# A backward pass with a state-space convolution and a feed-forward: the feed-forward spread more thinly over the table chain, one fold earlier, and two groups of loads further ahead

## The chip, the cores and the metric

The kernel runs on one core of one Trainium2 chip. The metric is the device time of one execution in microseconds (us), smaller is better. The engines are called PE (TensorE), DVE (VectorE), ACT (ScalarE), POOL (GpSimd) and SP (SyncE, here only an issuer of transfers); PEld is PE's loading of weights. To evacuate a result is to copy it out of the buffer in which PE left it. The granted clock is the share of its full speed that PE was given, and the DMA share is the mean busy share of the core's 16 DMA engines. L422 is line 422 of that kernel's source; the change adds lines.

## The reference, cut to what matters

The forward function is `x + s * silu(ffn(xn))`, where `xn` is the layer norm of `x`, `s` is a long convolution of `xn` with taps made from a diagonal state-space model, and `ffn` has two matrix products around a silu. The kernel returns the output and the gradients for the eleven differentiated inputs.

```python
def _A_ref(u, A_re, A_im, B_re, B_im, C_re, C_im, log_dt, Dskip):   # u: 1 x 2048 x 512, 128 states
    logdA = dt * (A_re + 1j * A_im)
    P = jnp.exp(logdA[:, :, None] * l[None, None, :])
    K = jnp.einsum("dn,dnl,dn->dl", Cc, P, dB).real                 # the taps
    ...                                                             # y = irfft(rfft(u) * rfft(K)) + u * Dskip
def _B_ref(x, w1, w2):                                              # 512 -> 1792 -> 512
    h = _silu(jnp.einsum("bsd,df->bsf", x, w1))
    return jnp.einsum("bsf,fd->bsd", h, w2)
xn = _layernorm(x)
out = x + _A_ref(xn, ...) * _silu(_B_ref(xn, B_w1, B_w2))
_out, _vjp = jax.vjp(_f, A_u, ..., B_x)                             # and all gradients for grad_out
```

## The kernel before

The 512 channels are worked on in four blocks `b`. For each block, `gen_tables` makes sines (ACT `sn`), multiplies them (DVE `E`), contracts them on PE (`ps_k`, then `ps_e`) and stores the taps `Kd`. `gen_conv_x` and `gen_conv_fwd` then do the convolution as a two-stage Fourier transform on PE: a first stage from `TF` (L286), a transposition by DMA from `dA` to `dB`, a second stage from `F` (L297, L298), a product of the spectra on DVE (`cm`, `sp_in`), and an inverse of two stages (L310, L319), from which DVE makes `S_b`. All these are Python generators. The order in which their steps are drawn is the order in which instructions enter each engine's queue.

```python
LAG = 3
def dft_fwd(k, w8, U, ev):
    ...                                                     # first stage into ps_s1, ev() to A
        nc.sync.dma_start_transpose(B[:, c], A[:, c]...)    # dB <- dA
    for _ in range(LAG):
        yield                                               # steps of others come in between
    ...                                                     # second stage, matmuls on B
```

`paced` draws one step of the chain and `rate` steps of another generator. The feed-forward has 72 steps: 8 chunks, each with seven steps of the first layer (`ps_h`, 8 matmuls) and two of the second (`ps_o`, 14 matmuls).

```python
def chain():
    yield from woven([gen_tables(k, 0), gen_conv_x(k, 0)], [2, 1])
    for b in range(1, 4):
        yield from woven([gen_tables(k, b), gen_conv_x(k, b), gen_conv_fwd(k, b - 1)], [3, 1, 1])
ffn = gen_ffn_fwd(k)
paced(chain(), ffn, 0.62)
...
gates = gen_gate_rows(k, ...)                                # ds = grad * silu(ffn), and the gate's gradient
interleave([gen_conv_fwd(k, 3), ffn, gates], [1, 3, 1])      # the last convolution: "the hole"
...
paced(bwd, woven([ffb, out], [2, 1]), BR)                    # backward convolution
...
ssm = gen_ssm_bwd(k, sb)                                     # state-space backward
paced(ffb, ssm, SR)
run(out)
...
interleave([ssm, chained([gen_dw2(k, fw), gen_dw1(k, fw)]), after(8, gen_ln_bwd(k, fw))], [2, 1, 2])
```

The state-space backward begins with loads of six parameters by transposing DMA, then a fold of block 0 (`GE` loaded, 23 matmuls, `Gf`), then the transposed table `YT`; the first product `ps_v` needs `Gf` (through `Gb`) and `YT`.

```python
par = load_params(k, sb, 0, k.D)
...
gf[0] = ssm_fold(k, 0, sb)
yt[0] = ssm_turned(k, *groups[0], sb)
```

`gen_out` writes the output rows. Its buffer for `x` is single, and the load stands in the step that uses it. `gen_ln_bwd` loads one step ahead.

```python
x = pool.tile([P, 2, k.D], BF16, name="go_x", tag="go_x", bufs=1)
nc.sync.dma_start(x[:], k.x_v[:, 2 * c:2 * c + 2, :])
...
q, pend = [load(0)], None                                    # gen_ln_bwd
for c in range(n + 1):
    if c + 1 < n:
        q.append(load(c + 1))
```

## Time and profile before

The median was 732.17 us over four runs (731.42 to 733.55). The profiled execution spans 732.4 us with a granted PE clock of 0.931. These moments, read from the lists of the instructions that touch one tile, carry the argument:

| moment (start of the instruction) | us |
|---|---|
| last matmuls of the last table (`ps_e`) | 254.6 |
| load of the last taps (`Kb`) issued | 263.7 |
| last `S_b` (last convolution done) | 313.9 |
| first `ps_da` (feed-forward backward) | 320.4 |
| last `du_b` (backward convolution done) | 468.0 |
| first `ps_v` (state-space products) | 490.7 |
| last `ps_da` | 536.0 |
| last state-space sum (`psS` copied) | 669.9 |
| end | 732.4 |

The view of waits gives, for an engine and line, what it waited for, then total us, number of times, longest. In the chain (40 to 262 us) two of its lines for the kernel before are:

```profile
DVE E L422 <- ACT sn L419: 18.2, 8, 5.3
...
ACT Xr L44 <- PE ps_k L447: 10.1, 8, 4.1
```

A time line has start, duration, engine, source line, operation, result and operand, shapes, count, and in brackets the idle time just before and what ended it.

### The profile page before, as it was taken

The numbers are of one execution on the slowest core, as the hardware profiler recorded it, in microseconds if no ns is written. First come the engines' busy times: TensorE is split into PE (matmuls) and PEld (weight loads), VectorE is DVE, ScalarE is ACT, GpSimd is POOL, SyncE is SP. The second block draws the span as 40 slices with busy tenths as digits, with TensorE's granted clock in tenths as the row PEclk, the third lists the DMA queues.
The fourth block names the chain that finished last, engine by engine and source line by source line (L and its number), as shares of the span: only waits on it lengthen the run. The fifth ranks groups of instructions, "written<-read, shape, count | busy, mean of one in ns | idle before, by whom it ended". The sixth has DMA issues, their size and how long they took to land.

```text
span 732.4 us, 13901 instructions
## 1 busy us (share of the span) xinstructions
PE 598.3 (82%) x5459; PEld 430.0 (59%) x5500; DVE 551.6 (75%) x1070; ACT 495.8 (68%) x671; POOL 107.7 (15%) x180
## 2 busy tenths in 40 slices
PE   0768968869999965569798799978797978899895
PEld 0535646555675643456576576647576646566784
DVE  6969996959988859877895989756897897784100
ACT  6768858769889866949679596646746767561211
POOL 2172200000010025600000000000002103102210
PEclk9877989989999995869999999999999999999998
DMA  9877847769669976579987875589959999930782
GB/s 291 304 172 195 264 170 211 273 171 280 277 183 281 338 266 162 183 162 261 322 203 233 242 224 180 160 197 210 249 156 295 253 286 280 217 120 28 155 179 66
DMA packets 207042, 159.26 MB, mean 217 GB/s; under 512 B 129024, under 2 KB 185344, under 8 KB 203392
## 3 DMA queue, kind: packets, MB, share of 16 engines
q1 hardware_dynamic: 193856, 135.29, 69.4%
q0 software_dynamic: 6224, 18.10, 6.9%
q10 hardware_dynamic: 6896, 4.98, 2.2%
q8 instruction: 43, 0.70, 0.4%
q14 instruction: 23, 0.19, 0.1%
HBM read 65.14 MB, written 62.26 MB: 174 GB/s over the span
## 4 chain that ended last, share of the span: by engine, by line
issue 52%; DVE 5%; POOL 5%; DMA 3%; PE 0%; ACT 0%; POOLq 0%; ACTq 0%; SPq 0%; DVEq 0%
POOL out_dram L939 1%; DMA out_dram<-gout 1%; DMA out_dram<-o 1%; DVE YD L599 1%; POOL out_dram L816 1%; DMA Kd<-KE 1%; DMA Gr<-in_grad_out_dram 1%; DVE ds L595 1%; DVE sp_in L332 1%; POOL out_dram L631 1%; POOL out_dram L958 1%; POOL out_dram L996 1%; POOL g L598 0%; DVE YD L603 0%; DVE YD L601 0%
## 5 line engine op out<-in xcount | busy, mean ns | idle before, releaser
L44 ACT CAST dA<-ps_s 128x1024 bf16<-128x1024 f32 x96 | 94.4, 1038 | 22.5 <-PE ps_s L286 13.2
L893 PE MATMUL ps_da<-doT,W 128*128 128x256 bf16 x448 | 62.7, 286 | 5.1 <-ACT doT L44 2.9
L541 PE MATMUL ps_h<-XT,W 128*128 128x256 bf16 x448 | 63.5, 293 | 1.5 <-ACT hT L44 0.8
L310 PE MATMUL ps_i<-I,sp_in 128*128 128x256 bf16 x384 | 53.4, 284 | 13.4 <-ACT dK L44 7.2
L558 PE MATMUL ps_o<-W,aT 128*128 128x512 bf16 x209 | 54.7, 394 | 4.1 <-ACT aT L549 2.9
L44 ACT CAST o<-ps_w 128x256 bf16<-128x256 f32 (+1 forms) x42 | 18.5, 441 | 57.2 <-PE ps_w L954 41.7
L44 ACT CAST dB<-ps_i 128x1024 bf16<-128x1024 f32 x48 | 47.2, 1025 | 12.0 <-PE ps_i L310 9.7
L746 DVE TENSOR_TENSOR Tp<-Vb,Eb 128x1344 bf16<-128x1344 bf16 x64 | 52.3, 852 | 3.3 <-PE psS L762 3.2
L893 PEld LDWEIGHTS <-W 128*128 128x128 bf16 x448 | 45.3, 103 | 16.0 <-issue 6.3
L904 PE MATMUL ps_dx<-W,dhT 128*128 128x512 bf16 x224 | 54.6, 383 | 0.0
L541 PEld LDWEIGHTS <-W 128*128 128x128 bf16 x448 | 46.1, 105 | 13.2 <-issue 2.8
L310 PEld LDWEIGHTS <-sp_in 128*128 128x128 bf16 x384 | 37.2, 101 | 28.2 <-DVE sp_in L333 9.4
L936 PE MATMUL ps_w<-YD,a_tok 128*128 128x512 bf16 x210 | 52.1, 394 | 1.2 <-issue 0.4
L954 PE MATMUL ps_w<-dh_tok,xn 128*128 128x256 bf16 x448 | 50.4, 273 | 1.8 <-DMA dh_tok<-DHd 1.3
L895 DVE SCALAR_TENSOR_TENSOR dhT<-dhT,ps_da 128x512 bf16<-128x512 bf16 x56 | 37.4, 681 | 17.7 <-PE ps_da L893 17.6
L954 PEld LDWEIGHTS <-xn 128*128 128x128 bf16 x448 | 43.3, 98 | 7.7 <-issue 2.8
L44 ACT CAST Vb<-ps_v 128x672 bf16<-128x672 f32 x64 | 42.3, 723 | 8.1 <-PE ps_v L736 8.1
L286 PEld LDWEIGHTS <-TF 128*128 128x128 bf16 x384 | 27.6, 106 | 28.2 <-issue 17.3
L419 ACT ACTIVATE sn<-V 128x1024 bf16<-128x1024 int32 (+3 forms) x40 | 34.8, 887 | 7.7 <-DVE V L417 7.4
L298 PE MATMUL ps_s<-dB,F 128*128 128x512 bf16 x95 | 37.9, 405 | 2.5 <-DMA dB<-dA 1.7
L297 PE MATMUL ps_s<-dB,F 128*128 128x512 bf16 x87 | 34.9, 408 | 5.8 <-DMA dB<-dA 4.1
L447 PEld LDWEIGHTS <-YD 128*128 128x128 bf16 x512 | 24.3, 101 | 23.9 <-DVE YD L434 12.8
(220 smaller groups left out, 1367.4 us busy)
## 6 DMA issues: line engine op xcount, KB each, us to landing
Yd<-YD SPq DMA_DIRECT2D x8, 1024.0 KB, 5.8
sp_in<-Ud SPq DMA_DIRECT2D x8, 1024.0 KB, 7.9
h_in<-Hd SPq DMA_DIRECT2D x14, 512.0 KB, 5.0
Ed<-E SPq DMA_DIRECT2D x8, 672.0 KB, 5.0
Eb<-Ed SPq DMA_DIRECT2D x8, 672.0 KB, 5.7
Hd<-hT POOLq DMA_DIRECT2D x8, 512.0 KB, 6.9
Ud<-dA SPq DMA_DIRECT2D x4, 1024.0 KB, 9.3
KXd<-dA SPq DMA_DIRECT2D x4, 1024.0 KB, 6.4
```

What stands on the lines that cost most here:

```text
L44: return self.nc.scalar.copy(out=out, in_=in_)
L297: nc.tensor.matmul(out=ps[:, 4 * u:4 * u + 4], lhsT=F2[:, m0], rhs=B[:, 0, g0:g0 + 4, :], start=True, stop=False)
L298: nc.tensor.matmul(out=ps[:, 4 * u:4 * u + 4], lhsT=F2[:, m1], rhs=B[:, 1, g0:g0 + 4, :], start=False, stop=True)
L310: nc.tensor.matmul(out=ps[:, g], lhsT=Y[:, c, g0 + g, :], rhs=k.I2[:, c].rearrange("p c m -> p (c m)"), start=(c == 0), stop=(c == 1))
L541: nc.tensor.matmul(out=ps[:, j], lhsT=k.W1[:, dk, ft * P:ft * P + P], rhs=XTv[:, :, dk, :], start=(dk == 0), stop=(dk == DK - 1))
L558: nc.tensor.matmul(out=ps[:], lhsT=aT[:, ft, t * P:t * P + P], rhs=k.W2[:, ft, :], start=(ft == 0), stop=(ft == FT - 1))
L746: k.nc.vector.tensor_tensor(out=Tp[:, c, :, r ^ c].rearrange("p e (q w) a -> p q w e a", w=2), in0=Vb[:, :, c].rearrange("p q w (e a) -> p ...
L893: nc.tensor.matmul(out=ps[:, j], lhsT=k.W2[:, ft, dk * P:dk * P + P], rhs=dTv[:, :, dk, :], start=(dk == 0), stop=(dk == DK - 1))
L895: nc.vector.scalar_tensor_tensor(out=dh[:, i0:i0 + 2, :], in0=dh[:, i0:i0 + 2, :], scalar=1.0, in1=ps[:], op0=ALU.add, op1=ALU.mult)
L904: nc.tensor.matmul(out=ps[:], lhsT=dhs[ft // 8][:, ft % 8, t * P:t * P + P], rhs=k.W1[:, :, ft * P:ft * P + P], start=(ft == 0), stop=(ft ...
L936: nc.tensor.matmul(out=ps[:], lhsT=at[:, t, :], rhs=k.do[:, t, :], start=(t == 0), stop=(t == k.T - 1))
L954: nc.tensor.matmul(out=ps[:], lhsT=k.xn[:, t, dk * P:dk * P + P], rhs=dh[:, t].rearrange("p j n -> p (j n)"), start=(t == 0), stop=(t == k ...
```

## The change

Its intent: (1) PE is nearly full in the table chain and has gaps in the hole, so less of the feed-forward is drawn in the chain and its last chunks run beside the last convolution; (2) the fold of block 0 is done earlier, inside the backward convolution, so that the state-space backward does not start with a wait for it; (3) the `x` load is issued one step earlier; (4) the loads of the layer norm's backward run two ahead, with a third `Gt` buffer.

```diff
-BR, SR = 1.8, 0.5
+BR, SR, FOLD = 1.8, 0.5, 28
 ...                                              # gen_out
+    def load_x(c):
+        x = pool.tile([P, 2, k.D], BF16, name="go_x", tag="go_x", bufs=1)
+        nc.sync.dma_start(x[:], k.x_v[:, 2 * c:2 * c + 2, :])
+        return x
     q = [load(0), load(1)]
+    x = load_x(0)
     yield
     for c in range(n):
         S, g = q.pop(0)
-        x = pool.tile([P, 2, k.D], BF16, name="go_x", tag="go_x", bufs=1)
-        nc.sync.dma_start(x[:], k.x_v[:, 2 * c:2 * c + 2, :])
 ...
         k.st(k.o0_v[:, 2 * c:2 * c + 2, :], x[:])
+        if c + 1 < n:
+            x = load_x(c + 1)
 ...                                              # gen_ssm_bwd (GE and Gf get other pools in ssm_fold)
-    gf[0] = ssm_fold(k, 0, sb)
+    gf[0] = k.gf0
 ...                                              # gen_ln_bwd
-        Gt = lw.tile([P, 2, D], BF16, name="Gt", tag="Gt", bufs=2)
+        Gt = lw.tile([P, 2, D], BF16, name="Gt", tag="Gt", bufs=3)
 ...
-    q, pend = [load(0)], None
+    q, pend = [load(0), load(1)], None
     for c in range(n + 1):
-        if c + 1 < n:
-            q.append(load(c + 1))
 ...
+        if c + 2 < n:
+            q.append(load(c + 2))
 ...
-    paced(chain(), ffn, 0.62)
+    paced(chain(), ffn, 0.5)
 ...
-    paced(bwd, woven([ffb, out], [2, 1]), BR)
+    def bwd_and_fold():
+        for i, _ in enumerate(bwd):
+            if i == FOLD:
+                k.gf0 = ssm_fold(k, 0, None)
+            yield
+    paced(bwd_and_fold(), woven([ffb, out], [2, 1]), BR)
```

More of the change, by code (lines that the diff above doesn't have):

```diff
@@ L684, in ssm_fold @@
     nc, pc = k.nc, k.pc
-    GE = sb.tile([P, 8, 8, 32], BF16, name="GE", tag="GE", bufs=1)
+    GE = sb.tile([P, 8, 8, 32], BF16, name="GE", tag="GE", bufs=1) if sb else k.dft.tile([P, 8, 8, 32], BF16, name="GE", tag="cm2")
     for a in range(4):
@@ L698, in ssm_fold @@
         z1 += [(ID, GE[:, 1, t, :], (1, 1, 2)), (ID, GE[:, 2:4, t, :], (1, 3, 5))]
-    Gf = sb.tile([P, 32, NE, 4], BF16, name="Gf", tag="Gf", bufs=2)
+    Gf = (sb if b % 2 else k.sf).tile([P, 32, NE, 4], BF16, name="Gf", tag="Gf", bufs=1)
     for bank, terms in ((0, z0), (1, z1)):
@@ L1131 @@
     k.dftb = SimpleNamespace(tile=lambda shape, dt, name, tag: base.tile(shape, dt, name=name, tag=next(turn) if tag == "w8" else tag))
+    k.sf = pool("sf", es=es_d)
     da = pool("da", es=es_d)
@@ L1145 @@
     es_d.close()
-    fw = pool("fw")
+    fw = k.sf = pool("fw")
     interleave([ssm, chained([gen_dw2(k, fw), gen_dw1(k, fw)]), after(8, gen_ln_bwd(k, fw))], [2, 1, 2])
```

## The prediction

> **What bounds the kernel now.** I read the page first, then busy time by stage, then each engine's time line around the gaps. On the page no engine is saturated, but TensorE comes nearest, and the 40 slices show where the two closest are loose together.
>
> ```profile
> PE 598.3 (82%) x5459; PEld 430.0 (59%) x5500; DVE 551.6 (75%) x1070; ACT 495.8 (68%) x671; POOL 107.7 (15%) x180
> ...
> PE   0768968869999965569798799978797978899895
> ...
> DVE  6969996959988859877895989756897897784100
> ...
> PEclk9877989989999995869999999999999999999998
> ```
>
> Each digit is a slice of 18.3 us. Slices 14 to 17 (256 to 330 us) are the hole: PE at 5 to 6 tenths, its clock down to 5. The last three slices have almost no VectorE work: the kernel ends with TensorE alone, on the weight gradient that nothing else needs. So time saved before that tail moves the tail forward in full. By stage (start:end, length, then busy us of PE, PEld, DVE, ACT, POOL, clock, DMA share, GB/s):
>
> ```profile
> 20.00:258.00 238.00, 200.69 (x1817) 137.11 (x1838) 202.07 (x420) 190.09 (x287) 36.13 (x45) 0.92 0.78 239
> 160.00:254.00 94.00, 89.82 (x854) 62.29 (x864) 84.03 (x163) 84.26 (x125) 9.59 (x12) 0.98 0.92 276
> 258.00:323.00 65.00, 37.94 (x292) 26.52 (x292) 52.91 (x72) 47.42 (x48) 28.74 (x17) 0.72 0.65 187
> 323.00:470.00 147.00, 132.76 (x1111) 95.35 (x1114) 121.90 (x173) 108.86 (x114) 6.83 (x12) 0.95 0.81 232
> 470.00:505.00 35.00, 28.87 (x267) 20.93 (x266) 21.39 (x30) 18.93 (x23) 0.00 (x0) 1.00 0.90 192
> ...
> 562.00:660.00 98.00, 86.18 (x868) 60.00 (x878) 83.03 (x212) 66.33 (x95) 18.24 (x34) 0.97 0.94 235
> 660.00:732.00 72.00, 60.43 (x569) 50.44 (x568) 10.40 (x40) 13.63 (x34) 13.75 (x23) 0.96 0.49 109
> ```
>
> The table chain (20 to 258) carries nearly the whole feed-forward; from 160 to 254 PE is busy 89.8 of 94 us, so it is the bound there. The last convolution with the gates (258 to 323) leaves PE 27 us idle; DVE is busiest, with 52.9 of 65. 323 to 470 is the backward convolution, close to PE-bound. 470 to 505 starts the state-space backward and has 6 us of PE idle and 13.6 of DVE. Two places carry the argument: ACT's time line in the hole, and DVE's where the first fold is awaited.
>
> ```profile
> 267.01 2.02 ACT L594 ACTIVATE YD<-YD 128x1024 bf16<-128x1024 bf16 x2
> 273.65 1.06 ACT L593 ACTIVATE g<-YD 128x1024 bf16<-128x1024 bf16 x1 [4.62 <-DVE YD L599]
> 274.62 0.57 ACT L44 CAST ob<-ps_o 128x512 bf16<-128x512 f32 x1
> 275.08 1.93 ACT L44 CAST dA<-ps_s 128x1024 bf16<-128x1024 f32 x2
> ```
>
> ```profile
> 481.96 0.28 DVE L780 TENSOR_TENSOR g_dBi<-dt,par_Bi 128x128 f32<-128x128 bf16 x1
> 489.11 3.03 DVE L714 TENSOR_TENSOR Gb<-Gf,MK 128x2688 bf16<-128x2688 bf16 x2 [6.87 <-ACT Gf L706]
> ```
>
> Bracketed is idle time before the line and what ended it. In the first, the convolution's evacuation dA stands behind a gate's silu that waits for DVE, though its matmuls were done by 269. In the second, DVE stands 6.87 us until the fold's result Gf exists.
>
> **What the Trainium skill says.** "TensorE: Matmul & The Clock Gate", Part 1 (the HAM clock gate): an idle PE array falls to half rate and needs a stretch of activity to return. The trace agrees: the same 32 inverse matmuls took 1.95 us at 257 and 3.51 us at 306, in the hole. "Perfetto Trace Analysis", per-engine timelines: ACT and DVE are strict FIFO. The dA line above is that. "SBUF — State Buffer", Who interferes with whom: DVE and GpSimd take a shared port pair as an exclusive lock. The gates' multiply L599 took 1.52 us beside GpSimd's tensor_scalar and 0.68 without, so gates in the hole are dearer than their size. "DMA: Bandwidth & Descriptors", Rules for kernel authors: issue early, wait late; go_x is issued just in time, landed 2.9 to 6.5 us after issue, and DVE waited 7.2 us on it in all.
>
> **The change, part by part.** The instruction counts are the same; the order moves. I compared the built order of both kernels, which a scheduler decides.
>
> (1) *Feed-forward at 0.5 instead of 0.62 steps per chain step.* The chain has 111 steps: 68 of the 72 feed-forward steps ran inside it, now 55. In the built order, ahead of the last table's final matmuls (254.9 us before), PE has 392 instead of 448 first-layer matmuls, 176 instead of 196 second-layer, and 17 small ones fewer. Busy per matmul is 63.5/448 = 0.142 and 54.7/209 = 0.262 us: 56 x 0.142 + 20 x 0.262 + about 1.8 = 15.0 us less. ACT has 7 evacuations (0.59), two silus (1.9 and 1.5) and two more evacuations (0.58) fewer: 8.7 us. DVE loses about nothing. The removal is spread over the chain. Where PE is bound (160 to 254), about 10 of the 15 us lie, and I count 8.5 of them, because DVE at 84 of 94 us takes over soon. Before 160 PE is at 67 to 82% in its slack slices and waits for DVE's tables; of 5 us there I count 1.5. The last table should be done **10 us earlier**.
>
> What is moved goes into the hole: 14 us of first and second layer there instead of 7, into 27 us of idle. But it isn't all beside other work. In the new order the last chunk's 28 second-layer matmuls (7.3 us) stand between the first 4 and the remaining 13 second-stage matmuls of the last convolution, behind the turning of W1, whose three-deep PSUM buffers need DVE and ACT. Walking the order with measured durations, from the last table: Kd lands and Kb is loaded at +14.5 us (before +13); dA is evacuated by +20 (before +25, since four dA now stand ahead of the blocked silus: 5 us won); then W1's turns and the 28 matmuls push the second stage's end to +40 to 43 (before +38). DVE's remaining 22 us of spectrum product and gates follow as before. The backward convolution starts at +65 to 69 instead of +65.5: I count a **loss of 3**. PE stays warmer there, but PE does not bound the stage.
>
> (2) *Fold of block 0 inside the backward convolution.* It moves 4 small loads, 23 matmuls (about 2 us), two ACT copies (1.86 and 0.69) to a place where the data landed long ago. It takes from the path: loads, fold, copies, up to the 6.87 us of DVE idle. The first ps_v at 490.7 then waits only for YT, issued at 481.5 behind six parameter transposes (8.2 us of queue), so about 484 to 485. PE already filled most of the gap with feed-forward backward work; its idle of 470 to 505 was 6 us. I count **4** of the 6.
>
> (3) *x load one ahead in gen_out.* Removes at most the 7.2 us of DVE wait in a stage where PE is 90% busy: **1.5**. The queue must still wait for the store before reloading the one buffer (21.1 us in six waits before); that wait only moves.
>
> (4) *Loads two ahead in the norm's backward.* DVE waited 11.4 us on pd_l, three times. DVE is 83 of 98 us there, but the tail after it is PE alone: **0.5**.
>
> Sum: 10 - 3 + 4 + 1.5 + 0.5 = 13 us, 732.8 - 13 = about **719.5 us**.
>
> **The rivals.** *A: the hole swallows the gain.* It is a latency chain (Kd, Kb, two transposes, product, inverse) with a full DVE, and the second layer now stands in its middle. For it: DVE busy 52.9 of 65. Against: ACT unblocks earlier and PE has 27 us free. If the hole grows by 10, the total is 727. *B: the chain is PE-bound throughout and gives back all 15,* the hole shrinks by 5 because dA and Gr come sooner, and the fold brings 6: about 706. For it: 89.8 of 94. Against: DVE at 84 of 94, and a chain whose early slices wait for DVE and DMA. *C: the fold and loads bring nothing,* because PE's in-order queue after 470 was already full: fold work only changes place, the queue of SP waits for YT instead, and the kernel lands at 725. For it: PE had 28.9 of 35 busy. Against: DVE's clear 6.87.
>
> **Range and chances.** Terms: chain 10 plus or minus 4, hole -3 plus or minus 5, fold 4 plus or minus 3, loads 2 plus or minus 2: together about 7 us. Eight in ten: 710 to 730. Two per cent is 718.1, just 1.4 us under the middle, so 0.42 for faster; slower by 2% would take all rivals at once, 0.02; the rest 0.56.
>
> **What would show it.** The last table's matmuls end at 243 to 248 instead of 254.9; later than 250 breaks the chain term. The first ps_da starts 63 to 70 us after it. The hole's clock is above 0.72, PE idle in it falls from 27 to about 20. The wait of Gb for Gf at the first group is gone and the first ps_v starts within 18 us of the last inverse matmul of the backward convolution (24 before). DVE's go_x wait is near 0. From the last sum of the state-space part to the end it stays 62 to 63 us (669.7 to 732.4 before). Wrong would be: second-layer matmuls in the hole at half rate pushing ps_da past +75, or a new wait of the SP queue ahead of YT or dB.

## More of the kernel before

DVE of the kernel before in the third block:

```profile
173.56 1.28 DVE L417 TENSOR_SCALAR V<-V 128x1024 int32<-128x1024 int32 x2
175.37 0.76 DVE L422 TENSOR_TENSOR E<-sn,mag 128x512 bf16<-128x512 bf16 x2 [0.52 <-ACT sn L419]
```

DVE waits only 0.52 us for the sine there. PE of the kernel before in the second stage of the last convolution, its end and the first inverse matmuls:

```profile
285.00 1.06 PE L297 MATMUL ps_s<-dB,F 128*128 128x512 bf16 x2
...
293.56 0.38 PE L298 MATMUL ps_s<-dB,F 128*128 128x512 bf16 x1
297.04 1.21 PE L310 MATMUL ps_i<-I,sp_in 128*128 128x256 bf16 x4 [3.10 <-DVE sp_in L333]
```

The second stage takes from 285.0 to 293.9, and the inverse then waits 3.10 us for the spectrum product.

## The result, and the profile after

The changed kernel took 744.13 us (median of four runs, 742.69 to 744.62) against 732.17 us. The ratio is 1.0158, with a 95% interval of 1.0135 to 1.0181: slower by 1.6%, outside the predicted range. A ratio here is the mean time of one kernel's fast runs over that of the other's fast runs of the same rounds, so it is not quite the ratio of the medians. All runs of both were fast (a run over 1.5% above the fastest of the same kernel would be called slow and left out).

| moment | before | after | difference | predicted difference |
|---|---|---|---|---|
| last table's matmuls | 254.6 | 259.2 | +4.6 | -10 |
| `Kb` issued | 263.7 | 265.9 | +2.2 | |
| last `S_b` | 313.9 | 322.0 | +8.1 | |
| first `ps_da` | 320.4 | 329.7 | +9.3 | -7 |
| last `du_b` | 468.0 | 477.2 | +9.2 | |
| first `ps_v` | 490.7 | 495.2 | +4.5 | |
| last `ps_da` | 536.0 | 544.4 | +8.4 | |
| last state-space sum | 669.9 | 679.8 | +9.9 | -12.5 |
| end | 732.4 | 742.0 | +9.6 | -13 |

In these two profiles 4.6 us are lost in the chain and as much again in the hole. Each is one profile; how far other profiles of the same order differ is said with the run pace_lag6. The backward convolution neither loses nor wins. The fold wins 4.7 us at the first `ps_v`, and by the last state-space sum that is gone. The page of the kernel after, busy times and the three rows by slice:

```profile
PE 599.8 (81%) x5459; PEld 435.1 (59%) x5500; DVE 551.5 (74%) x1070; ACT 496.7 (67%) x671; POOL 101.5 (14%) x180
...
PE   0678968866959888569779999969997886999995
...
DVE  6969996866996955988777989857888798794200
...
PEclk9878989999998997669989999989999998999999
```

The busy times of PE, DVE and ACT are the same to within 0.3%. Counting slices from 0, numbers 9 to 13 (about 165 to 260 us) show PE at 6 9 5 9 8 where before they showed 9 9 9 9 9: PE is no longer dense there. DVE, at 6 9 9 6 9 where it had 9 9 8 8 8, has become no denser either. By stage (start:end, length, busy us of PE, PEld, DVE, ACT, POOL, clock, DMA share, GB/s), with the windows moved along:

```profile
258.00:330.00 72.00, 51.08 (x435) 37.67 (x436) 51.37 (x71) 57.54 (x70) 25.11 (x20) 0.78 0.65 181
330.00:477.00 147.00, 132.95 (x1127) 96.38 (x1130) 122.30 (x175) 113.38 (x117) 6.83 (x12) 0.95 0.82 231
477.00:513.00 36.00, 27.17 (x211) 18.41 (x210) 24.07 (x32) 17.69 (x21) 0.00 (x0) 0.91 0.88 184
...
570.00:670.00 100.00, 88.60 (x895) 63.03 (x907) 84.95 (x213) 68.76 (x98) 18.25 (x34) 0.97 0.94 241
670.00:742.00 72.00, 60.59 (x569) 50.37 (x568) 10.40 (x40) 13.64 (x34) 13.76 (x23) 0.98 0.50 109
```

In the hole PE's idle time fell to 20.9 us and the clock rose to 0.78, both as predicted, and yet the stage is longer.

**Where the chain loses.** The chain's waits, after:

```profile
DVE E L422 <- ACT sn L419: 30.8, 9, 6.1
ACT Xr L44 <- PE ps_k L447: 14.8, 12, 4.0
```

DVE waits 12.6 us more for the sines. One step of it can be followed back through three engines in the third block. First PE:

```profile
172.18 0.61 PE L297 MATMUL ps_s<-dB,F 128*128 128x512 bf16 x1 [2.70 <-DMA dB<-dA]
...
173.86 1.26 PE L447 MATMUL ps_k<-W,YD 128*128 128x84 bf16 x15
174.91 0.42 PE L541 MATMUL ps_h<-XT,W 128*128 128x256 bf16 x1
176.85 0.38 PE L298 MATMUL ps_s<-dB,F 128*128 128x512 bf16 x1 [1.52 <-DMA dB<-dA]
...
178.47 0.77 PE L447 MATMUL ps_k<-W,YD 128*128 128x84 bf16 x16
```

PE stops 2.70 and 1.52 us for the transposed `dB`, and the tables' `ps_k`, whose operands do not depend on `dB`, stand behind those matmuls. Then ACT, which evacuates both:

```profile
175.16 0.44 ACT L44 CAST Xr<-ps_k 128x336 bf16<-128x336 f32 x1 [2.67 <-PE ps_k L447]
177.70 1.01 ACT L44 CAST dA<-ps_s 128x1024 bf16<-128x1024 f32 x1 [2.10 <-PE ps_s L298]
178.61 1.06 ACT L419 ACTIVATE sn<-V 128x1024 bf16<-128x1024 int32 x1
```

The next sine stands behind them. And DVE, which stood still the longest:

```profile
179.70 0.76 DVE L422 TENSOR_TENSOR E<-sn,mag 128x512 bf16<-128x512 bf16 x2 [5.60 <-ACT sn L419]
```

This is 5.60 us where the kernel before had 0.52. The Trainium skill, "PSUM — Partial Sum Buffer", Engine vs sequencer instructions, says that matmuls start and complete in program order. The trace agrees: no `ps_k` passed the waiting L298, which held PE to 176.85. In the built order the kernel before has all 64 `ps_k` of this table half ahead of the second stage of the block's second convolution, with feed-forward work in between; its trace reaches that stage only at 179.34:

```profile
179.34 0.38 PE L297 MATMUL ps_s<-dB,F 128*128 128x512 bf16 x1
```

In the kernel after, less feed-forward is drawn between them, and that stage begins (at 172.18) behind the first `ps_k`, ahead of the other 63.

**Where the hole loses.** PE of the kernel after in the second stage of the last convolution:

```profile
285.13 0.58 PE L297 MATMUL ps_s<-dB,F 128*128 128x512 bf16 x1 [0.62 <-DMA dB<-dA]
...
287.98 6.21 PE L558 MATMUL ps_o<-W,aT 128*128 128x512 bf16 x28
294.02 0.38 PE L297 MATMUL ps_s<-dB,F 128*128 128x512 bf16 x1
...
306.59 3.77 PE L310 MATMUL ps_i<-I,sp_in 128*128 128x256 bf16 x16 [6.77 <-DVE sp_in L333]
```

On ACT the moved order works as predicted: the four evacuations `dA` are no longer stuck behind a silu.

```profile
272.40 3.77 ACT L44 CAST dA<-ps_s 128x1024 bf16<-128x1024 f32 x4
```

So the second stage begins at the same moment as before (285.1) although the tables were 4.6 us later; but the last chunk's 28 second-layer matmuls cut it in two, and the inverse starts at 306.59 instead of 297.04. The wait for `sp_in` in these lines is not itself the loss: in the run null, which is the kernel before again, it is 5.94 us and not 3.10. What differs beyond that scatter is where the stage ends, counted from the issue of `Kb` (32.2 us after it, before 30.2), and the time from there to the last `S_b` (23.9 us, before 20.0).

**Where the fold's win goes.** PE after, at the first `ps_v` (L736 of the kernel before is L742 of the kernel after), and SP's queue before it:

```profile
495.19 0.46 PE L742 MATMUL ps_v<-Gb,YT 128*128 128x168 bf16 x2 [6.82 <-DMA YT<-Yd]
```

```profile
481.18 2.07 SPq L346 DMA_TRANSPOSE par_Ar<-in_A_A_re_dram  x1
...
488.54 1.26 SPq L346 DMA_TRANSPOSE par_Ci<-in_A_C_im_dram  x1
489.84 2.66 SPq L731 DMA_TRANSPOSE YT<-Yd  x2
```

The wait of DVE for `Gf` at this place has gone, and a wait of PE for `YT` of nearly the same size has come: `YT` is issued behind six parameter transposes. The `x` load did not help either; DVE's wait for it after the change is

```profile
DVE go_x L634 <- DMA go_x<-in_A_u_dram: 8.2, 3, 3.8
```

where it was 7.2 us in two waits before.

### The profile page after: what moved, and what is told of

It reads as the page before. It is cut to its first block, busy times and chain, and to the rows that moved or that the text cites. A ratio compares the mean times of both kernels' runs of the same rounds, so it can differ in the third digit from the quotient of the medians.

```text
span 742.0 us, 13903 instructions
## 1 busy us (share of the span) xinstructions
PE 599.8 (81%) x5459; PEld 435.1 (59%) x5500; DVE 551.5 (74%) x1070; ACT 496.7 (67%) x671; POOL 101.5 (14%) x180
## 4 chain that ended last, share of the span: by engine, by line
issue 52%; DVE 17%; ACT 10%; DMA 10%; PE 5%; POOL 4%; ACTq 0%; POOLq 0%; SPq 0%; DVEq 0%
ACT dA L44 4%; DMA dB<-dA 2%; ACT sn L419 2%; DMA out_dram<-o 2%; PE ps_o L558 2%; DVE W L442 2%; DVE E L422 1%; DMA Ud<-dA 1%; DMA Kd<-KE 1%; DVE YD L434 1%; DVE V L414 1%; DVE m L433 1%; DMA mag<-Md 1%; DVE V L417 1%; ACT KE L44 1%
## 5 line engine op out<-in xcount | busy, mean ns | idle before, releaser
L44 ACT CAST dA<-ps_s 128x1024 bf16<-128x1024 f32 x96 | 93.2, 1038 | 23.9 <-PE ps_s L286 17.8
L310 PEld LDWEIGHTS <-sp_in 128*128 128x128 bf16 x384 | 37.6, 102 | 30.2 <-DVE sp_in L333 13.9
L942 PE MATMUL ps_w<-YD,a_tok 128*128 128x512 bf16 x210 | 49.4, 379 | 0.7
L297 PE MATMUL ps_s<-dB,F 128*128 128x512 bf16 x87 | 34.1, 397 | 9.9 <-DMA dB<-dA 6.7
L422 DVE TENSOR_TENSOR E<-sn,mag 128x512 bf16<-128x512 bf16 (+1 forms) x48 | 18.9, 432 | 30.8 <-ACT sn L419 30.8
L742 PE MATMUL ps_v<-Gb,YT 128*128 128x168 bf16 x256 | 28.9, 244 | 11.7 <-DMA YT<-Yd 8.3
## 6 DMA issues: line engine op xcount, KB each, us to landing
Ed<-E SPq DMA_DIRECT2D x8, 672.0 KB, 4.2
Eb<-Ed SPq DMA_DIRECT2D x8, 672.0 KB, 5.9
```

What stands on the lines that cost most here:

```text
L44: return self.nc.scalar.copy(out=out, in_=in_)
L297: nc.tensor.matmul(out=ps[:, 4 * u:4 * u + 4], lhsT=F2[:, m0], rhs=B[:, 0, g0:g0 + 4, :], start=True, stop=False)
L310: nc.tensor.matmul(out=ps[:, g], lhsT=Y[:, c, g0 + g, :], rhs=k.I2[:, c].rearrange("p c m -> p (c m)"), start=(c == 0), stop=(c == 1))
L942: nc.tensor.matmul(out=ps[:], lhsT=at[:, t, :], rhs=k.do[:, t, :], start=(t == 0), stop=(t == k.T - 1))
```

## The experiments

Eighteen kernels were run, each correct. Kernels are compared only within the same rounds. Those chips spread more than the one of the first measurement (the kernel before ran between 726.8 and 741.5 us on them), so the intervals are about 0.4% either way. The ratios leave out slow runs: two of the kernel before (739.05 and 739.55 us), one each of lag6_h312 and best_fold. The stretch below is from the issue of the last `Kb` to the last `S_b`; "steps ahead" counts feed-forward steps (of 72) that stand ahead of the last table's matmuls in PE's built order; it does not count the turns of W1, which are drawn with the last chunk. The moments are from one profile each.

| kernel | steps ahead | last table | `Kb` | last `S_b` | stretch | last `du_b` | ratio to before, 95% |
|---|---|---|---|---|---|---|---|
| before | 70.0 | 254.6 | 263.7 | 313.9 | 50.2 | 468.0 | 1 |
| null | 70.0 | 255.7 | 263.6 | 314.2 | 50.6 | 463.4 | 0.9994 (0.995 to 1.0037) |
| whole change | 61.6 | 259.2 | 265.9 | 322.0 | 56.1 | 477.2 | 1.0158 (1.0135 to 1.0181) |
| pace_only | 61.6 | 256.1 | 263.2 | 318.9 | 55.7 | 471.3 | 1.0138 (1.0086 to 1.019) |
| pace_lag6 | 64.5 | 250.2 | 262.3 | 318.2 | 55.9 | 474.6 | 1.0136 (1.0084 to 1.0189) |
| pace_hole5 | 61.6 | 257.0 | 263.7 | 319.6 | 55.9 | 472.2 | 1.009 (1.0045 to 1.0136) |
| h161 | 61.6 | 256.6 | 263.4 | 321.5 | 58.1 | 473.7 | 1.0098 (1.0056 to 1.0141) |
| h211 | 61.6 | 259.1 | 265.8 | 311.5 | 45.7 | 478.6 | 1.0126 (1.0084 to 1.0168) |
| pace_h312 | 61.6 | 257.4 | 263.8 | 311.2 | 47.4 | 479.1 | 1.0156 (1.012 to 1.0193) |
| lag6_h312 | 64.5 | 250.0 | 261.9 | 306.0 | 44.1 | 455.9 | 0.9886 (0.9844 to 0.9929) |
| pace68 | 72.0 | 266.5 | 274.8 | 323.7 | 48.9 | 475.6 | 1.0122 (1.0078 to 1.0165) |
| best_62 | 72.0 | 261.3 | 268.8 | 318.6 | 49.8 | 480.8 | 1.0176 (1.0134 to 1.0218) |

### One part at a time

**pace_only**: the rate alone.

```diff
-    paced(chain(), ffn, 0.62)
+    paced(chain(), ffn, 0.5)
```

> The kernel before with the feed-forward's pace 0.5 and nothing else. Its built TensorE order up to the first feed-forward backward matmul is that of the changed kernel. Theory 1 (the pace is the whole loss: with less feed-forward between them, second-stage matmuls that wait for DMA transposes stand ahead of the table matmuls, and the wait spreads to ACT and DVE): last table's matmuls at 258 to 260 us instead of 254.9, first ps_da at 328 to 331 instead of 320.4, and the end 8 to 11 us late, 741 to 744. Rival (the fold, the loads or their buffers cost as much as the pace): ps_da as above or not, but the total at 734 to 738.

Measured: 742.22 us, ratio 1.0138. The pace alone is slower and accounts for most of the whole loss: the last `S_b` comes 5.0 us late and the end of the profiled run 5.9 us late. The last table (256.1) and the first `ps_da` (326.7) came a little before the expected ranges.

**fold_only**: the early fold alone.

```diff
-    gf[0] = ssm_fold(k, 0, sb)
+    gf[0] = k.gf0          # made at step 28 of the backward convolution, GE and Gf in other pools
```

> The kernel before with the early fold alone. If the fold's saving is real and carried to the end: first ps_v 4 to 5 us earlier (486 instead of 490.7) and the total 727 to 729. If it only turns into a wait for YT, which is issued behind six parameter transposes: ps_v earlier by 4 to 5, TensorE idle of 5 us or more ahead of it put down to YT, and a total of 731 to 735.

Measured: 738.62 us, ratio 1.0084 (1.0034 to 1.0134). The first `ps_v` starts at 483.7, 7.0 us earlier than before, with the last `du_b` within a microsecond of before (467.3). It waited 6.10 us for `YT`. The last state-space sum is nevertheless at 672.0 (669.9 before), and the time is above both expectations.

**loads_only**: the `x` load and the layer norm's loads alone (the two parts of the diff above).

> The kernel before with x loaded one chunk ahead in the forward output and the norm's loads two ahead, nothing else. If DVE's waits for go_x (7.2 us) and pd_l (11.4 us) were on the path: 725 to 730. If hidden, or only moved to the queue that waits for the store: 731 to 735, with the waits of DVE for go_x and pd_l still 15 us or more together.

Measured: 738.96 us, ratio 1.0093 (1.0032 to 1.0154). DVE waited 8.2 us for `pd_l` (11.4 before) and 5.8 us for `go_x` (7.2 before), and the time lies above both expectations. The fall of the second is not shown: in the run null, without any change, that wait was 4.7 us. The four kernels of this call share one set of runs of the kernel before. With its two slow runs kept, each ratio would be about 0.2% lower, so a small loss stays.

**fold_yt**: the early fold, and the parameter loads moved behind the first `YT`.

```diff
-    par = load_params(k, sb, 0, k.D)
-    par["dt"] = k.dt[:]
     ...
     gf[0] = k.gf0
     yt[0] = ssm_turned(k, *groups[0], sb)
+    par = load_params(k, sb, 0, k.D)
+    par["dt"] = k.dt[:]
```

> Early fold alone, and the first two YT transposes issued ahead of the six parameter transposes (8 us of queue time) instead of behind them. If the queue's order is what the fold's saving ran into: first ps_v 6 to 9 us earlier than in fold_only, the 5 to 7 us wait of TensorE for YT gone, and the total 3 to 7 us under fold_only. If the stage is bound elsewhere (VectorE, or the rest of the state-space chain): ps_v earlier but the total within 2 us of fold_only.

Measured: 739.37 us, ratio 1.0095 (1.0043 to 1.0147). PE of this run at the first `ps_v`:

```profile
479.08 0.32 PE L736 MATMUL ps_v<-Gb,YT 128*128 128x168 bf16 x2 [1.87 <-DMA YT<-Yd]
```

This is 9.4 us after the last `du_b` (469.7), against 22.7 before and 16.4 in fold_only. So the queue behind the parameters was the new wait. But removing it as well bought nothing: the last state-space sum is at 671.0. The start of the state-space products is not what sets the end of that part.

**all_but_pace**: the whole change with the rate put back to 0.62.

> The whole change but with the pace at 0.62: early fold and further-ahead loads. Each alone gave a ratio of 1.008 to 1.009 on another chip run. If the two losses are separate they add: ratio 1.016 to 1.019, time about 745 to 747. If they are one and the same (the queue of SyncE, or the placing of transfers, disturbed once), the ratio is 1.007 to 1.011. If the whole change's loss is the pace's alone and the single figures were the spread of that chip, the ratio is 0.995 to 1.004.

Measured: 740.05 us, ratio 1.0059 (1.0015 to 1.0102). Its last `S_b` is at 313.8, as before. Fold and loads together lose no more than either alone, as far as the intervals tell, so the single losses do not add.

### Does the order on PE carry the loss of the pace?

**pace_lag6**: pace 0.5, and six steps instead of three between the transposes and the second stage of the convolutions in the chain.

```diff
-def dft_fwd(k, w8, U, ev):
+def dft_fwd(k, w8, U, ev, lag=LAG):
 ...
-    for _ in range(LAG):
+    for _ in range(lag):
 ...
-    U, _ = yield from dft_fwd(k, dft, lambda t: k.xn[:, t, bs], k.evc)
+    U, _ = yield from dft_fwd(k, dft, lambda t: k.xn[:, t, bs], k.evc, 6)
 ...
-    KX, A2 = yield from dft_fwd(k, dft, lambda t: Kb[:, :, t, :], k.evc)
+    KX, A2 = yield from dft_fwd(k, dft, lambda t: Kb[:, :, t, :], k.evc, 6 if b < 3 else LAG)
```

> Pace 0.5 alone, but in the chain six steps instead of three lie between the transposes of a convolution and the matmuls of its second stage, so that in the built order the second-stage matmuls of the third block stand behind the table's first matmuls. Theory (order on TensorE): the tables were late because those matmuls waited for transposes in front of them, so the last table ends at 250 or earlier instead of 256 (pace alone) and 259 (the whole change), and the end comes 4 to 7 us before that of pace alone (742): 735 to 738. Rival (the chain is bound by ScalarE and VectorE and the order on TensorE does not matter): the last table still ends at 256 to 259 and the time stays at 740 to 744; the longer convolution may even make it later.

Measured: 744.12 us, ratio 1.0136. The first half of the theory holds: the last table comes at 250.2, 5.9 us earlier than in pace_only, and DVE's wait for the sines in the chain falls from 27.1 to 19.8 us (18.2 before). That happened although 2.9 more feed-forward steps stood ahead of it, because the longer wait makes more chain steps. The view of waits (40 to 262 us), first pace_only, then pace_lag6:

```profile
DVE E L422 <- ACT sn L419: 27.1, 9, 6.0
```

```profile
DVE E L422 <- ACT sn L419: 19.8, 6, 5.9
```

These are single profiles, but more kernels settle it. Up to the last table, six kernels each share one built order on PE: that of before (with null, fold_only, fold_yt, loads_only, all_but_pace), that of pace 0.5 (pace_only, the whole change, pace_hole5, h161, h211, pace_h312), and that of pace 0.5 with six steps (pace_lag6 and five kernels further below). Their last tables came at 253.1 to 255.9, at 256.1 to 259.2 and at 248.1 to 253.0 us, and DVE's waits for the sines were 17.8 to 18.9, 26.1 to 30.8 and 18.6 to 21.1 us. So the order of pace 0.5 stands clear of both others, beyond the scatter; those two nearly touch in the last table's moment. On average the thinner pace made the last table 2.7 us later, not 4.6, and six steps made it 7.1 us earlier than that. Part of the latter is not the wait: 16 more matmuls of a convolution's inverse, 1.9 us, now stand behind the last table.

The second half fails: the last `Kb` is issued only 0.9 us earlier and the stretch is still 55.9 us. The list of the `Kd` tile gives the time from issue to landing of the last four `Kd` stores, minimum, median and maximum; in the kernel before (252 to 262 us):

```profile
DMA to landing us min/median/max: 3.9/4.9/5.6
```

and in pace_lag6 (248 to 258 us):

```profile
DMA to landing us min/median/max: 7.2/7.5/7.8
```

The stores landed 2.6 us slower than in the kernel before (median), beside four `Gr` loads for the gates that SP issued from 253.7 on; between the last table and `Kb` the DMA share was 1.01 here and 0.60 before.

**pace_hole5**: pace 0.5, weight 5 for the feed-forward in the hole.

```diff
-    interleave([gen_conv_fwd(k, 3), ffn, gates], [1, 3, 1])
+    interleave([gen_conv_fwd(k, 3), ffn, gates], [1, 5, 1])
```

> Pace 0.5 alone, with the feed-forward given weight 5 instead of 3 in the interleave with the last convolution and the gates, so that its remaining steps run earlier in that stretch, ahead of the second stage's matmuls. Theory (the place of the remaining chunks matters): the stretch from the last table to the first ps_da falls from 70.6 us (pace alone) to 66 to 68, before had 65.8, and the time falls by 3 to 4 us to about 738. Rival (it is the work as such: every matmul moved in here lies on the path to ps_da): the stretch stays at 70 to 71 us and the time at 741 to 744.

Measured: 742.4 us, ratio 1.009. The stretch from the last table to the first `ps_da` was 72.3 us (70.6 in pace_only). This run did not test what it was made for: in the built order the 28 matmuls still stand inside the second stage, behind its first matmul. It only says that moving the first layer ahead does not help.

**pace68**: the rate the other way, 0.68.

> The pace moved the other way, 0.68 instead of 0.62, nothing else of the change: all feed-forward steps then lie inside the chain and none is left for the last convolution. Theory (filler between a transpose and its consumer keeps TensorE from waiting): the last table ends within 2 us of before's 254.6, the stretch to the first ps_da is 61 to 64 us instead of 65.8, and the time is 1 to 3 us under that of before. Rival (TensorE's busy time in the chain is what counts, as the prediction had it): the last table ends 4 us later, at 258 to 260, and the time is the same as before or up to 3 us over it.

Measured: 743.96 us, ratio 1.0122. Both theories miss. The stretch is the short one (48.9), but the last table comes at 266.5, 11.9 us later than before (the profile is that of the slowest of its six runs). Only two more steps stand ahead of it, but these are 28 matmuls of the second layer (7.3 us by the prediction's durations), and with them come 50 more turns of W1, which the count of steps leaves out. PE was busy 205.5 us from 20 us to the last table, where it had been 197.8, so about two thirds of the delay is plain work, as the prediction would count it. Work added where PE is dense does cost time; that the same amount is won when work is taken away is what failed.

### The kernel before against itself

**null**: only a comment was added.

> The kernel before itself, with nothing but a comment added. Each of eight variants, in both directions of the pace, came out 0.6 to 1.4 per cent slower on the noisier chips. If that is partly a bias of the comparison or the spread of the chip, this run is slower too, ratio 1.004 to 1.010, and the small losses of the fold and the loads (1.006 to 1.009) are not real. If the comparison is fair the ratio is 0.996 to 1.003 and those losses are real.

Measured: 731.85 us, ratio 0.9994. In this call the comparison is fair (the other calls had no such control); a single kernel moves a profile by some 3 us (729.2 here, 732.4 in the first), which is why single profiles are used here for moments inside a stage and not for the end.

### Where the moved chunk stands in the hole

**h211** and **h161**: pace 0.5 with weights 2, 1, 1 and with 1, 6, 1.

```diff
-    interleave([gen_conv_fwd(k, 3), ffn, gates], [1, 3, 1])
+    interleave([gen_conv_fwd(k, 3), ffn, gates], [2, 1, 1])      # h211
+    interleave([gen_conv_fwd(k, 3), ffn, gates], [1, 6, 1])      # h161
```

> Pace 0.5 alone, and the stretch of the last convolution interleaved with weights 2, 1, 1 instead of 1, 3, 1, so that the last chunk's 28 second-layer matmuls (7.6 us) stand behind the convolution's inverse instead of in the middle of its second stage. The stretch from the load of the last taps (Kb) to the last S_b was 50.2 us before and 55.7 to 56.1 in all kernels with pace 0.5. Theory (those 28 matmuls in front of the second stage's last ones are the loss): 49 to 52 us here, though the last gates, which wait for that chunk, may then end later than S_b and give part of it back after. Rival (it is the sum of the work, whatever its place): 55 to 57 us again.

> Pace 0.5 alone with weights 1, 6, 1: the 28 second-layer matmuls now stand ahead of the whole second stage, between the halves of the first stage. Theory (the place counts): the second half of the first stage, and so the transposes, come some 7 to 8 us later, and the stretch from Kb to the last S_b is 56 us or longer, up to 62. Rival (they fill idle time of TensorE while it waits for the transposes, so ahead is the right place): 50 to 53 us. The pair with weights 2, 1, 1 tells which side, if any, is right.

Measured: h211 744.35 us (1.0126), h161 739.33 us (1.0098). Busy time from `Kb` to the last `S_b`, first pace_only, then h161, then h211 and its backward convolution:

```profile
263.20:318.90 55.70, 38.37 (x341) 26.79 (x340) 41.78 (x55) 44.78 (x50) 25.07 (x20) 0.84 0.63 189
```

```profile
263.40:321.50 58.10, 39.04 (x347) 27.07 (x345) 45.87 (x62) 47.56 (x52) 23.93 (x20) 0.85 0.60 181
```

```profile
265.80:311.50 45.70, 28.83 (x261) 20.84 (x259) 41.53 (x55) 35.21 (x40) 19.75 (x17) 0.81 0.63 187
311.50:478.60 167.10, 143.44 (x1233) 102.43 (x1232) 133.25 (x192) 127.20 (x131) 10.19 (x15) 0.96 0.76 220
```

With the 28 matmuls behind the inverse the stretch falls by 10 us, with them between the halves of the first stage it grows by 2.4 us: the place counts, as the theory said. (The weights move the gates too, so the 10 us are not the 28 matmuls' alone; no run moves these matmuls by themselves.) What h211 wins is then lost, and PE shows how:

```profile
309.96 6.21 PE L558 MATMUL ps_o<-W,aT 128*128 128x512 bf16 x28
...
323.49 0.61 PE L286 MATMUL ps_s<-ds,TF 128*128 128x128 bf16 x8 [0.31 <-ACT dA L44]
```

The first transform of the backward convolution reads `ds`, which needs the gate of the last rows, which needs these 28 matmuls; 32 turns of W2 (2.0 us) stand behind them in PE's order as well. It ends at 324.1, 12.6 us after the last `S_b`; before it ended at 318.4, 4.5 us after. The chunk moved into the hole has a deadline of its own.

**lag6_h312**: both repairs, pace 0.5, six steps of wait, weights 3, 1, 2.

```diff
-    interleave([gen_conv_fwd(k, 3), ffn, gates], [1, 3, 1])
+    interleave([gen_conv_fwd(k, 3), ffn, gates], [3, 1, 2])      # and the diff of pace_lag6
```

> The two repairs together: pace 0.5, six steps between transposes and second stage in the chain (the last table ended at 250.2 with that, against 254.6 before), and weights 3, 1, 2 in the last stretch, which keep the 28 second-layer matmuls out of the last convolution's second stage. Theory: last S_b at 311 to 314 (318.2 with the first repair alone, 313.9 before), time within 2 us of before, 730 to 737 on a chip where before has 735. Rival (the gain at the tables is worthless because the load of the last taps does not follow it, 262.3 against 263.7 before, and the last stretch costs 5 us anyway): last S_b at 317 to 320, time 5 us over before.

Measured: 725.63 us against 732.99, ratio 0.9886 (0.9844 to 0.9929): faster than both kernels. Between the last table and `Kb`, then from there to the last `S_b`:

```profile
250.00:261.90 11.90, 8.37 (x77) 6.94 (x75) 5.53 (x8) 7.81 (x17) 0.90 (x1) 1.00 1.03 341
261.90:306.00 44.10, 31.52 (x274) 22.33 (x273) 37.85 (x49) 35.74 (x39) 20.36 (x17) 0.80 0.63 189
```

and PE at the moved chunk:

```profile
285.90 0.38 PE L298 MATMUL ps_s<-dB,F 128*128 128x512 bf16 x1
...
286.56 3.19 PE L558 MATMUL ps_o<-W,aT 128*128 128x512 bf16 x14
289.59 0.38 PE L310 MATMUL ps_i<-I,sp_in 128*128 128x256 bf16 x2
```

The second stage is whole and over by 286.3. Half of the 28 matmuls run just behind it, while DVE makes the spectrum product, and the other half stand among those of the inverse. The inverse starts 3.3 us after the second stage, as before (3.1; 5.9 in null), where the changed kernel needed 8.5. The last `S_b` comes 5 us earlier than the theory said; how much of that is the place of the chunk, and how much the other weight of the gates, no run separates. The DMA share of 1.03 in the first line is the same crowding as in pace_lag6, and it still eats most of the 4.6 us won at the tables: `Kb` is issued only 1.8 us earlier than before. Most of the gain is made in the hole, where the stretch is 44.1 us instead of 50.2.

### What was left open: the pace by itself, one repair alone, the fold and the loads

**best_62**: both repairs with the old rate of 0.62.

> The two repairs (six steps between transposes and second stage in the chain; weights 3, 1, 2 in the last stretch) on the kernel before with its old pace of 0.62, so nothing of the change itself. Because the longer wait makes more steps in the chain, all 72 feed-forward steps then lie in it (70.0 before, 64.5 with pace 0.5 and both repairs). Theory (thinning does pay once the order is right): the last table ends at 254 or later, the ratio to before is 0.995 to 1.005, so worse than the 0.9886 with pace 0.5. Rival (the repairs do it all and the pace was never worth anything): last table by 251, ratio 0.985 to 0.991.

Measured: 747.62 us, ratio 1.0176. The repairs without the pace are worse than before, worse also than the theory said: the last table comes at 261.3 instead of 250.0. With the longer wait the chain has more steps, so all 72 feed-forward steps went ahead of the last table. The 11.3 us for 7.5 steps look like the prediction's 15 us for 8.4, but 73 turns of W1 and W2 went ahead with them, as in pace68, and the order changed too.

**pace_h312**: weights 3, 1, 2 and pace 0.5 without the longer wait.

> Pace 0.5 with weights 3, 1, 2 but without the longer wait in the chain. The built order has the 28 second-layer matmuls of the last chunk behind the convolution's inverse, as with 2, 1, 1 (which lost 1.3 per cent: last S_b 311.5, but the backward convolution 13 us longer). Theory (both repairs are needed): last table at 256 to 259, last S_b at 308 to 312, then the last gates wait for that chunk and the time is 738 to 745, ratio 1.006 to 1.014. Rival (the weights alone carry the gain): ratio 0.985 to 0.995.

Measured: 745.36 us, ratio 1.0156, with the last `S_b` at 311.2 and the last `du_b` at 479.1: the same loss in the backward convolution as h211. One repair alone does not pay. Without the longer wait too much of the feed-forward (10.4 steps, not 7.5) is left for the hole, and its second layer again stands behind the inverse.

**best_all** and **best_fold**: both repairs on the whole change, and on the pace and the fold without the loads.

> The whole change (pace 0.5, early fold, further-ahead loads) with both repairs. If fold and loads cost what they cost on the kernel before (ratio 1.006 together), the ratio is 0.992 to 0.997; if they are worth nothing either way it is that of the repairs and the pace alone, 0.986 to 0.991; if the fold pays now, 0.980 to 0.985.

> Pace 0.5, both repairs and the early fold, without the loads. Set beside the run with everything, on the same chip, it tells the loads' part: if these are what costs, this one is faster by 0.3 to 0.9 per cent; if it is the fold, the two are within 0.3 per cent and both 0.4 to 0.9 per cent slower than without the fold (0.9886). The first ps_v comes within 16 to 18 us of the last du_b either way (24 with pace and repairs alone).

Measured: best_all 730.6 us, 0.9945 (0.9906 to 0.9984); best_fold 726.96 us, 0.9886 (0.9846 to 0.9926). So the fold is neutral beside lag6_h312 (0.9886, on another chip). Its local win is there again, the first `ps_v` 15.9 us after the last `du_b` (23.8 in lag6_h312), and is given back again: from the last `du_b` to the last state-space sum it takes 204.7 us against 206.1. The loads look like a loss of 0.6%, with intervals that overlap.

**best_fold_x** and **best_fold_ln**: best_fold with only the `x` load moved, and with only the layer norm's loads moved.

> Pace 0.5, both repairs, early fold, and of the loads only the x load of the output rows moved one step ahead, still in its one buffer. VectorE waited for go_x 7.2 us in the kernel before but not at all in the same kernel without this part, so there is nothing left to win. Theory (a load that waits for its single buffer's store holds up the queue of SyncE behind it, so this part carries the loss of both loads, 0.6 per cent): ratio 0.993 to 0.997. Rival (it is the layer-norm loads that cost): ratio 0.986 to 0.991, as without it.

> The same kernel with, of the loads, only those of the layer-norm backward ahead by two with a third Gt buffer. They run beside the last stage, whose end is set by the weight gradients, so theory: neutral, ratio 0.986 to 0.991. Rival (they come into the queues while the state-space part needs its own loads, and cost the 0.6 per cent): ratio 0.992 to 0.997, with the stretch from the last ps_da to the last state-space sum 2 us or more above the 138 us without them.

Measured: 729.35 us, 0.9952 (0.9903 to 1.0001), and 726.81 us, 0.992 (0.9875 to 0.9966). Inconclusive: the `x` load alone lies at the ratio of best_all (0.9945), the norm's loads halfway to best_fold (0.9886), and all four intervals overlap. Neither load is shown to gain, and which of the two costs, if one does, stays open. A second `x` buffer, which would have freed that load from its store, was not run: with it the kernel does not build, as one pool lacks room in the on-chip memory (it needs 86.5 kB per partition where 84.7 are left).

## Why the prediction was wrong, point by point

**The chain term, "The last table should be done 10 us earlier", is the step that failed.** It measured +4.6 us (+2.7 on average over the six kernels of each order). Its working counted the PE busy time that the thinner pace removes, and took it as time won where PE was dense. The busy time did go, though not "spread over the chain": up to 160 us PE was busy 107.3 us before and 108.0 after, from there to the last table 90.4 and 79.7. But the filler had a second use: it stood between a transpose and the matmuls that wait for it. Without it the waiting matmuls held up the tables' `ps_k` in PE's order, then ACT's `Xr` and `sn`, then DVE's `E`. pace_lag6 shows this cause: with the same pace and a longer distance between transpose and user, the last table came at 250.2, and in all six kernels with that order it came before those of both other orders. The prediction named "later than 250 breaks the chain term" as its test, and 259.2 broke it. None of its rivals for the chain saw this; they only asked who else would be full.

**The hole, "I count a loss of 3".** From the last table to the first `ps_da` it took 70.5 us instead of 65.8, a loss of 4.7, just past the "63 to 70 us" that was to be seen; with the old pace and order six profiles gave 64.6 to 67.0. The mechanism was right in its first half: the 28 matmuls cut the second stage (behind its first 3 of 16 matmuls in the built order; the prediction's 4 and 13 do not add up to 16), PE was idle 20.9 us, and the clock was 0.78. But counted from the last table the stage did not end later, at 38.9 us where 40 to 43 were walked and the kernel before had 39.3. What was mis-sized is what follows: "DVE's remaining 22 us of spectrum product and gates follow as before". From the end of the stage to the first `ps_da` it took 31.6 us instead of 26.5 (26.5 to 27.3 in the six). h161, h211 and lag6_h312 show that the placing of the chunk and the gates moves this stretch. Why the part behind the stage became longer stays open: in h211 no matmul of the chunk stands inside the stage, and its last `S_b` still comes 22.9 us after the stage's end (before 20.0), so the gates that share DVE with the product are a rival that no run isolates.

**The fold, "I count 4 of the 6".** Right where it was looked for: 4.7 us at the first `ps_v`, 18.0 us after the last `du_b`. Wrong as a gain: none of it is left at the last state-space sum. Rival C had said it ("the queue of SP waits for YT instead") and the run showed exactly that wait. fold_yt goes further: with that wait mostly gone too, the time stays. So the step from "ps_v earlier" to "end earlier" failed. Why that stage gives it back is argued, not shown: PE is busy 57.9 + 118.6 = 176.5 us of the 201.9 us from the last `du_b` to the last state-space sum in the kernel before, and the fold takes no PE work away.

**The loads, 1.5 and 0.5.** Neither came. DVE's wait for `go_x` went from 7.2 to 8.2 us (null had 4.7, so its size is mostly scatter), and SP's wait for the store of that buffer was 21.1 us in both kernels. The prediction had itself written that the wait for the single buffer's store "only moves", and still counted 1.5.

**The tail** behaved as predicted: 62.2 us from the last state-space sum to the end. Rivals A (727) and C (725) each pointed the right way about their own stage, but neither doubted that the chain would become shorter, and that is why the range ended below the result.

## What to carry to other kernels

Before filler is thinned on an in-order engine, look at what stands on both sides of it: filler between a transfer and its user is a delay that someone needs, and the gain must be read from the new built order (does a waiting instruction now stand ahead of the critical one?), not from the busy time removed. Work moved into a gap needs a place as well as room: here the same 28 matmuls cost 5 us inside a transform, 13 us after the stretch when placed behind it, and nothing visible when half stood just after the second stage and half among the inverse's matmuls (with the gates moved as well). A start moved earlier is worth nothing until it is shown that the stage's end follows it.

## What the Trainium skill lacked or had wrong

Nothing that was used was found wrong. Lacking were:

- "Perfetto Trace Analysis", Optimization Strategy, advises interleaving regimes with different limits. It does not say that the place of the interleaved work on the in-order engine can outweigh its amount: at pace 0.5 the stretch was 58.1, 55.7, 45.7 or 44.1 us by place, and with 61.6 steps ahead of it the last table came later (256.1 to 259.2 us in six kernels) than with 70.0 (253.1 to 255.9 in six).
- "DMA: Bandwidth & Descriptors", Rules for kernel authors, advises issuing early. It does not add that a load into a single buffer cannot come before that buffer's store has landed: SP's wait for that store was 21.1 us before and 21.1 us after the issue was moved ahead.
- The same page has a figure for the latency of HBM under load, but none for how much longer a small store takes to land beside large loads: here the last four `Kd` stores took 4.9 us (median) where the DMA share was 0.60 and 7.5 us where it was 1.01.
